# One row table for two mixture layers, and the first expert's first two slots made up in mid-attention

## The chip, the cores and the metric

The kernel runs on one NeuronCore of a Trainium2 chip. Its engines are TensorE (PE: matmuls, and the loads of their stationary operand, PEld), VectorE (DVE), ScalarE (ACT), GpSimd (POOL) and SyncE (SP), which only issues DMAs here; 16 DMA engines move the data. The metric is the device time of one execution in microseconds (us); of the kernel before there are three timed runs and one profiled execution.

## The reference

Three stages follow one another: attention with capped scores, a mixture of experts whose router knows the token's modality, and a second mixture without. Each token goes to one expert.

```python
scores = cap * np.tanh(scale * np.matmul(q, k.transpose(0, 1, 3, 2)) / cap)   # 4 batches, 12 heads, 448 tokens, 64 wide
attn = np.exp(scores - max); attn = attn / (attn.sum(-1, keepdims=True) + 1e-09)
x = np.matmul(attn, v)                       # then laid out as 1792 tokens x 768
# mixture 1 (mixture 2 is the same, without the bias)
logits = x @ w_gate + modality_bias[modality_id]
e_idx = np.argmax(logits, axis=1)            # 8 experts
gate_w = softmax(logits)[arange, e_idx]
for e in range(8):
    out[e_idx == e] = gate_w * (np.maximum(x[e_idx == e] @ w1[e], 0) @ w2[e])   # w1 768x1024, w2 1024x768
```

## The kernel before

**Attention.** Work goes by pairs of heads, 24 of them (4 batches x 6 pairs). `load(i)` issues five DMAs on SyncE for a pair: four pieces of Q and K into a tile `qkn` (pool `nat`, four buffers) and the values `vn`. In the loop over `i`, SyncE first gets the load of pair i+2. Then TensorE makes scores of pair i (L763, L767), ScalarE takes tanh and exp (L775, L777), and TensorE multiplies the exponentials of pair i-1 with its values (L811, L814) into the PSUM bank `po`, which VectorE copies to `ot` (L816). GpSimd and VectorE add up the exponentials (`presum`, `presum_last`). After each three pairs a `group` of tasks is put in a queue, one or two of which run between two pieces of a pair: the sums and router logits (L837), their transposes, the choice of expert, the rank of each token among its expert's tokens (`rank_a`), its place (`place_a`), and the transposes of `ot` into rows `xb`. `store` writes half of a batch's rows into a table in HBM, and `place_a` scatters token numbers by place into a list `td[0]`, so that the rows of an expert stand one after another there (four DMAs of 112 numbers from GpSimd, L963).

**Two row tables.** `xs[0]` takes the attention's rows, `xs[1]` the first mixture's results; each has 128 rows at its end that belong to no token. While the attention runs, SyncE copies such rows over the whole of `xs[1]` and over the last batch of `xs[0]` (L1004, L1007).

**Mixtures.** They go by slots: up to 128 tokens of one expert, gathered from the row table through the place list. A slot's x is transposed on TensorE (L329) and split into a high part `xh` and a low part `xl`; weights are split in the same way (`split_hi` on ScalarE, `split_lo` on VectorE or GpSimd, L285), and each product is three matmuls: high-high, high-low, low-high. `first(h, ks)` is the first layer for half h of the hidden width (L348 to L350), `second(h, ks)` the second (L368 to L370). While one slot is computed, the rows of the next are gathered (`load_tok` on SyncE, then `gather` on GpSimd, L323); `xg` holds one gathered tile.

**The junction.** The first expert is that of token 0, known after batch 0, and its weights come in mid-attention. `slot0` fills the expert's count up to 128 and loads its list after three batches, and its rows are gathered at the last pair. Behind the last pair's values, slot 0 is then computed piece by piece between the router steps of the last group, in an order written out by hand in the source. The place list gets the last batch there, and `slot_table` works out from the counts which expert and rows each slot has (`meta`, `nxt_i`, `beg_i`). `enter(0)` then loads the next expert's weights, finishes slot 0, transposes slot 1's x and gathers slot 2. All instructions of an engine run in this program order; each waits by semaphores. Of the DMAs that SyncE issues, each waits for the eighth before it.

Of the kernel before, what the change touches and what calls it, by code (L numbers as in the profile page):

```python
# [22 lines left out]
def tile_attention_two_moes(  # L23
# [37 lines left out]
    MAXS = NT + E  # L61
    SL = MAXS + 4
    LATE = 5
    FH = F // 2
# [10 lines left out]
    xs = [dram.tile([N + P, XW], F32, name=f"xs{l}") for l in range(2)]  # L75
# [12 lines left out]
    scol = cst.tile([P, 1], F32, name="scol")  # L88
    tokf = cst.tile([CP, B, NC], F32, name="tokf")
# [23 lines left out]
    def make_constants(tmp, none):  # L113
# [15 lines left out]
        iota(tokf, [[S, B], [1, NC]], 0, NC)  # L129
        iota(invf, [[0, 1]], N, 1)  # L130
        nc.gpsimd.iota(inv_i, pattern=[[0, ROWS // P + 1]], base=N, channel_multiplier=1)
        nc.gpsimd.iota(tok_i, pattern=[[S, B], [1, NC]], base=0, channel_multiplier=NC)
        iota(thr, [[P, NT]])
        iota(scol, [[0, 1]], 0, 1)
        iota(srow, [[1, SL + 1]])
# [10 lines left out]
        def none_rows():  # L146
            for l in range(2):
                nc.sync.dma_start(xs[l][N:N + P, :].rearrange("(p c) w -> p c w", c=NC), none)
                nc.sync.dma_start(td[l].rearrange("(p c) o -> p (c o)", p=P), inv_i)
# [20 lines left out]
    def fill_first(pool, cnt_ps, l, name):  # L170
# [8 lines left out]
        nc.vector.tensor_tensor(acc[l][0:1], acc[l][0:1], more, op=ALU.add)  # L179

# [122 lines left out]
    xg = cst.tile([P, XW], F32, name="xg")  # L303
    tk = cst.tile([P, 1], I32, name="tk")
    ti = cst.tile([P, 1], I32, name="ti")
# [13 lines left out]
    def gather(l, tk=tk, ti=ti):  # L319
        if tk is not None:  # L320
            nc.scalar.copy(ti, tk)
            pool_reads(ti)
        nc.gpsimd.indirect_dma_start(out=xg, out_offset=None, in_=xs[l],  # L323
                                     in_offset=bass.IndirectOffsetOnAxis(ap=ti, axis=0),
                                     bounds_check=N + P - 1, oob_is_err=False)
# [9 lines left out]
    def adopt(l, first=False):  # L335
        if not first:
            nc.vector.tensor_copy(gtc, gt1)
            if l:
                nc.vector.tensor_copy(tci, gtc[:, 1:2])
# [32 lines left out]
    def finish(l):  # L372
        nc.scalar.activation(yo[:, 0:DH], py[0][:, 0:DH], AF.Copy, scale=gtc[:, 0:1])  # L373
        nc.vector.tensor_scalar(yo[:, DH:D], py[1][:, 0:DH], gtc[:, 0:1], None, op0=ALU.mult)  # L374
        if l == 0:
            nc.vector.tensor_copy(tci, gtc[:, 1:2])
            nc.vector.tensor_copy(yo[:, D + 1:D + 2], gtc[:, 1:2])
            nc.vector.tensor_scalar(vm, gtc[:, 1:2], N - 0.5, None, op0=ALU.is_lt)
# [42 lines left out]
    def place(pk, gathered=False, copied=True):  # L421
# [5 lines left out]
        if gathered:  # L427
# [5 lines left out]
        nc.gpsimd.indirect_dma_start(out=xs[1], out_offset=bass.IndirectOffsetOnAxis(ap=t, axis=0),  # L433
                                     in_=y, in_offset=None, bounds_check=N - 1, oob_is_err=False)
# [191 lines left out]
    def enter(l):  # L626
# [4 lines left out]
        if l == 0:  # L631
            load_w1(0, e1, 2)
# [11 lines left out]
        with tc.If(reg(beg_i[l], 1, 1) == 1):  # L644
            for kk in range(KD):
# [629 lines left out]
```

## Time and profile before

| | us |
|---|---|
| median of the timed runs (lowest, highest) | 964.93 (962.68, 966.96) |
| profiled execution | 960.36 |
| its span, first to last instruction | 958.5 |
| TensorE busy (share of the span) | 902.5 (94%) |
| VectorE, ScalarE, GpSimd busy | 487.3 (51%), 432.8 (45%), 285.1 (30%) |
| mean granted clock of TensorE | 0.974 |

The page of the profile draws the span in 40 slices of 24 us. The first nine are attention, the tenth and eleventh hold its end and the first slots; the first mixture has 15 slots, the second 20. Each digit is the busy share of an engine in tenths; the row PEclk is the granted clock of TensorE, 1.0 being 2.4 GHz. In the 5th slice and around the 11th and 25th both TensorE and its clock are lower. The busy time of a stretch says little where several engines wait for one another; what ended each wait is in the lists of waits and in the order of time, of which the rows are below.

### The profile page before, as it was taken

The numbers are of one execution on the slowest core, as the hardware profiler recorded it, in microseconds if no ns is written. First come the engines' busy times: TensorE is split into PE (matmuls) and PEld (weight loads), VectorE is DVE, ScalarE is ACT, GpSimd is POOL, SyncE is SP. The second block draws the span as 40 slices with busy tenths as digits, with TensorE's granted clock in tenths as the row PEclk, the third lists the DMA queues.
The fourth block names the chain that finished last, engine by engine and source line by source line (L and its number), as shares of the span: only waits on it lengthen the run. The fifth ranks groups of instructions, "written<-read, shape, count | busy, mean of one in ns | idle before, by whom it ended". The sixth has DMA issues, their size and how long they took to land. (4 is left out here: it accounts for less than half of the span.)

```text
span 958.5 us, 15556 instructions
## 1 busy us (share of the span) xinstructions
PE 902.5 (94%) x4721; PEld 696.9 (73%) x4721; DVE 487.3 (51%) x1181; ACT 432.8 (45%) x666; POOL 285.1 (30%) x330
## 2 busy tenths in 40 slices
PE   8999899998599999999999985999999999999994
PEld 2333233334499899989989875899899989989984
DVE  3878468576633333394334564543612499952111
ACT  6787577785422222272222243533522488842121
POOL 7667457685412111112111220211111211211111
PEclk9999899998999999999999987999999999999998
DMA  8355998931574432275322335461811299981110
GB/s 186 99 182 125 149 297 153 287 46 47 68 260 54 37 46 34 34 205 135 45 37 35 53 85 194 138 248 36 311 38 35 77 337 375 370 330 35 51 51 20
DMA packets 59077, 128.11 MB, mean 134 GB/s; under 512 B 12920, under 2 KB 20072, under 8 KB 58602
## 3 DMA queue, kind: packets, MB, share of 16 engines
q1 hardware_dynamic: 51850, 100.68, 35.7%
q0 software_dynamic: 6960, 26.08, 13.8%
q14 instruction: 81, 0.66, 0.4%
q8 instruction: 42, 0.69, 0.3%
q10 hardware_dynamic: 144, 0.00, 0.0%
HBM read 109.27 MB, written 27.12 MB: 142 GB/s over the span
## 5 line engine op out<-in xcount | busy, mean ns | idle before, releaser
L368 PE MATMUL pb<-w2h,hh 128*128 128x384 f32 x560 | 193.6, 346 | 0.9 <-DVE meta L252 0.9
L369 PE MATMUL pb<-w2l,hh 128*128 128x384 f32 x560 | 189.0, 338 | 1.8 <-POOL w2l L285 1.6
L370 PE MATMUL pb<-w2h,hl 128*128 128x384 f32 x560 | 188.9, 337 | 0.0
L369 PEld LDWEIGHTS pb<-w2l,hh 128*128 128x128 f32 x560 | 106.2, 190 | 3.8 <-POOL w2l L285 2.0
L368 PEld LDWEIGHTS pb<-w2h,hh 128*128 128x128 f32 x560 | 106.2, 190 | 2.4 <-issue 1.2
L370 PEld LDWEIGHTS pb<-w2h,hl 128*128 128x128 f32 x560 | 106.0, 189 | 0.0
L775 ACT ACTIVATE tnh<-pa,rcap 128x896 f32<-128x896 f32 x72 | 70.0, 1005 | 53.4 <-PE pa L763 53.3
L361 DVE TENSOR_TENSOR hl<-pa,hh 128x512 fp32r<-128x512 f32 x34 | 23.5, 691 | 135.3 <-ACTq L480 130.2
L348 PE MATMUL po<-w1t,xh 128*128 128x512 f32 x210 | 87.8, 418 | 0.0
L348 PE MATMUL pa<-w1t,xh 128*128 128x512 f32 x210 | 85.4, 406 | 0.0
L349 PE MATMUL po<-w1t,xh 128*128 128x512 f32 x210 | 82.6, 393 | 1.6 <-DVEq L530 1.6
L349 PE MATMUL pa<-w1t,xh 128*128 128x512 f32 x210 | 83.6, 398 | 0.0
L350 PE MATMUL pa<-w1t,xl 128*128 128x512 f32 x210 | 83.4, 397 | 0.0
L350 PE MATMUL po<-w1t,xl 128*128 128x512 f32 x210 | 82.9, 395 | 0.0
L763 PE MATMUL pa<-qkn 64*128 64x448 f32 x288 | 71.5, 585 | 7.8 <-DMA qkn<-in_qk_dram 6.6
L777 ACT ACTIVATE prb<-tnh,capt 128x1792 f32<-128x1792 f32 (+1 forms) x48 | 77.0, 1604 | 3.2 <-ACT tnh L775 0.4
L373 ACT ACTIVATE yo<-pb,gtc 128x384 f32<-128x384 f32 x35 | 20.4, 583 | 121.2 <-PE pb L370 99.9
L285 DVE TENSOR_TENSOR w2l<-raw,w2h 128x768 fp32r<-128x768 f32 x77 | 70.4, 954 | 2.4 <-ACT w2h L279 1.7
L314 POOL TENSOR_TENSOR jki<-ti 128x1 int32<-128x1 int32 x35 | 7.5, 214 | 214.9 <-ACTq L516 128.1
L285 DVE TENSOR_TENSOR w1t<-raw,w1t 128x512 fp32r<-128x512 f32 x111 | 68.7, 687 | 3.1 <-ACT w1t L279 1.8
L314 POOL TENSOR_TENSOR jki<-pi 128x1 int32<-128x1 int32 x15 | 2.8, 184 | 226.5 <-DVE pi L424 175.3
L279 ACT ACTIVATE w1t<-raw 128x512 fp32r<-128x512 f32 x120 | 64.8, 623 | 0.4 <-ACTq L548 0.3
(287 smaller groups left out, 1560.7 us busy)
## 6 DMA issues: line engine op xcount, KB each, us to landing
raw<-in_w_dram SPq DMA_DIRECT2D x43, 1536.0 KB
qkn<-in_qk_dram SPq DMA_DIRECT2D x48, 128.0 KB
vn<-in_v_dram SPq DMA_DIRECT2D x24, 256.0 KB
xs<-xs SPq DMA_DIRECT2D x14, 385.0 KB
qkn<-in_qk_dram SPq DMA_DIRECT2D x48, 112.0 KB
xs<-xb SPq DMA_DIRECT2D x4, 672.0 KB
xs<-xb SPq DMA_DIRECT2D x3, 675.5 KB
xs<-xs SPq DMA_DIRECT2D x4, 336.9 KB
```

The costliest lines, as they stand in the source:

```text
L279: nc.scalar.activation(hi, raw[:, kk, :], AF.Copy)
L285: e.tensor_tensor(lo, raw[:, kk, :], hi, op=ALU.subtract)
L348: nc.tensor.matmul(ph[h], xh[:, kk, :], w1h(h, kk), start=kk == 0, stop=False)
L349: nc.tensor.matmul(ph[h], xh[:, kk, :], w1l(h, kk), start=False, stop=False)
L350: nc.tensor.matmul(ph[h], xl[:, kk, :], w1h(h, kk), start=False, stop=kk == KD - 1)
L361: nc.vector.tensor_tensor(hl[h], pt[h], hh[h], op=ALU.subtract)
L368: nc.tensor.matmul(o, hh[h][:, kk, :], w2h[h][:, kk, sl], start=h == 0 and kk == 0, stop=False)
L369: nc.tensor.matmul(o, hh[h][:, kk, :], w2l[h][:, kk, sl], start=False, stop=False)
L370: nc.tensor.matmul(o, hl[h][:, kk, :], w2h[h][:, kk, sl], start=False, stop=h == 1 and kk == 3)
L763: nc.tensor.matmul(ps[:, a, :], kn[r, ks], qn[r], start=True, stop=True)
L775: nc.scalar.activation(tv if w == 2 else tv[:, 0, :], ps, AF.Tanh, scale=rcap)
L777: nc.scalar.activation(p, t[:, 0:2 + w, :], AF.Exp, scale=capt)
```

## The change

- There is one row table `xs`: 128 rows of no token in front, then 1792 rows. The first mixture's results are written over the rows that the slots have read; gathers of the first mixture and these scatters are declared independent. The copies of L1004 and L1007 are gone, and token numbers in the lists are larger by 128.
- At pair 16 (`FILL`), `fill_two` fills the first expert's count up to two slots, from the two batches that have been placed. SyncE loads both lists at pair 17, GpSimd gathers slot 0 at pair 18, TensorE transposes it in pair 20 (`early_x`), and slot 1 is gathered at pair 21. Both gathers name only the rows of the first two batches.
- The first half of the first expert's w1 is split in pairs 15 to 20, one of six parts a pair, on ScalarE and VectorE; GpSimd splits no weights any more.
- `xh` and `xl` lie among the constants, and pool `nat` has three buffers instead of four. The last pair's values go to `po` like the others.
- The order between the last pair and slot 1 is written anew: three steps of the first layer come first; the slot table comes after the first layer. A slot more is allowed for (`MAXS`).

```diff
-    MAXS = NT + E
+    MAXS = NT + E + 1
+    FILL = 2 * NP + 4
-    xs = [dram.tile([N + P, XW], F32, name=f"xs{l}") for l in range(2)]
+    xs = dram.tile([P + N, XW], F32, name="xs")
+    read, written = [], []
...
+    def fill_two(pool, cnt_ps, name):
+        nc.tensor.matmul(cnt_ps, ones, acc[0], start=True, stop=True)
+        miss = pool.tile([2, E], F32, name=f"miss{name}")
+        nc.vector.tensor_scalar(miss, cnt_ps[0:2], -1.0, room, op0=ALU.mult, op1=ALU.add)
+        nc.vector.tensor_scalar(miss, miss, 0.0, float(P), op0=ALU.max, op1=ALU.min)
+        isf = pool.tile([2, E], F32, name=f"isf{name}")
+        nc.vector.tensor_scalar(isf, iota1[0:2], e1p[0][0:2], None, op0=ALU.is_equal)
+        more = pool.tile([2, E], BF16, name=f"more{name}")
+        nc.vector.tensor_tensor(more, miss, isf, op=ALU.mult)
+        nc.vector.tensor_tensor(acc[0][0:2], acc[0][0:2], more, op=ALU.add)
...
-    def gather(l, tk=tk, ti=ti):
+    def gather(l, tk=tk, ti=ti, rows=P + N):
...
+        if l == 0:
+            no_dep(d, written)
+            read.append(d.ins)
...
-        nat = early.enter_context(tc.tile_pool(name="nat", bufs=4))
+        nat = early.enter_context(tc.tile_pool(name="nat", bufs=3))
...
-                o_t[i] = (po if i < n - 1 else ph[0])[:, 0:S]
+                o_t[i] = po[:, 0:S]
...
+        def early_x(j):
+            if j:
+                adopt(0, True)
+            ks = slice(4 * j, min(4 * j + 4, KD))
+            w = ks.stop - ks.start
+            px = ps_t().rearrange("p (k c) -> p k c", c=P)[:, 0:w]
+            for kk in range(w):
+                nc.tensor.transpose(px[:, kk], xg[:, (4 * j + kk) * P:(4 * j + kk + 1) * P], ident)
+            nc.scalar.activation(xh[:, ks], px, AF.Copy)
+            nc.vector.tensor_tensor(xl[:, ks], px, xh[:, ks], op=ALU.subtract)
...
         for i in range(n):
             if i + 2 < n:
                 load(i + 2)
-            if 6 <= i < 6 + NT:
-                nc.sync.dma_start(xs[1][(i - 6) * P:(i - 5) * P, :], xs[0][N:N + P, :])
-                if i < 6 + NC:
-                    r = N - S + (i - 6) * CP
-                    nc.sync.dma_start(xs[0][r:r + CP, :], xs[0][N:N + CP, :])
+            if i == FILL + 1:
+                r0 = reg(row0_i[0], 0, ROWS - N, engines=SP)
+                load_tok(0, r0)
+                load_tok(0, r0 + P, tkb)
...
-                if i == n - NP + 1:
-                    def slot0():
-                        fill_first(rt, ps_t()[:, 0:E], 0, "a")
-                        load_tok(0, reg(row0_i[0], 0, ROWS - P, engines=SP))
-                    queue.append(slot0)
-            if i == n - 1:
-                gather(0, None, tk)
+            if i == FILL:
+                fill_two(rt, ps_t()[:, 0:E], "a")
+            if i == FILL + 2:
+                gather(0, None, tk, P + 2 * S)
+            if i == FILL + 5:
+                gather(0, None, tkb, P + 2 * S)
+            if 0 <= i - FILL + 1 < KD:
+                split_w1(0, i - FILL + 1)
...
+                if i == FILL + 4:
+                    early_x(c // 2)
...
-        x_transpose()
-        x_split()
-        adopt(0, True)
-        for kk in range(4, KD):
-            split_lo(raw1[0], w1h(0, kk), w1l(0, kk), kk, "p")
-        t_sums()
+        first(0, range(3))
         for kk in range(KD):
             split_hi(raw1[1], w1h(1, kk), kk, "a")
-        split_lo(raw1[1], w1h(1, 0), w1l(1, 0), 0, "v")
-        for kk in (1, 2, 3):
-            split_lo(raw1[1], w1h(1, kk), w1l(1, kk), kk, "p")
+        t_sums()
+        for kk in range(2):
+            split_lo(raw1[1], w1h(1, kk), w1l(1, kk), kk, "v")
...
-        first(0, range(2))
+        first(0, range(3, 5))
         t_scalars()
-        first(0, range(2, 4))
-        for kk in range(2):
-            split_hi(raw2[0], w2h[0][:, kk, :], kk, "a")
+        first(0, range(5, 6))
+        relu(0)
         rows_[0](True)
-        first(0, range(4, 6))
         choose_()
-        relu(0)
+        for kk in range(2, 4):
+            split_lo(raw1[1], w1h(1, kk), w1l(1, kk), kk, "v")
+        first(1, range(1))
...
+        for kk in range(4):
+            split_w2(0, kk)
+        first(1, range(3, 6))
         relu(1)
+        st = slot_table(mc, px[:, 6:8, :].rearrange("p a b -> p (a b)"), 0)
+        next(st)
+        second(0, range(1))
+        next(st)
+        second(0, range(1, 2))
+        h_transpose(1)
+        h_split(1)
```

What the change moves on TensorE behind the last pair. Before, from the last pair's values on (`pa_120` is their bank, `xg` slot 0's rows, the rows with `one_h`, `wgp` and `one_a` are the last group's sums):

```order
L811 MATMUL pa_120<-prb,vn 64x448 x6
L814 MATMUL pa_120<-prb,vn 128x448
L329 MATMUL pa_119<-ident,xg 128x128 x6
L837 MATMUL pb_122<-pst,one_h 32x448 x2
L837 MATMUL pb_122<-prb,one_h 32x448
L837 MATMUL pb_122<-ot,wgp 32x448 x2
L837 MATMUL pb_122<-psm,one_a 32x448 x2
L837 MATMUL pb_122<-ot,wgp 32x448
L348 MATMUL pa_120<-w1t_0_110,xh 128x512
```

And in the changed kernel, where the same lines have other numbers (L841 and L844 are the values, L375 to L377 the first layer, L867 the sums):

```order
L841 MATMUL po<-prb,vn 64x448 x6
L844 MATMUL po<-prb,vn 128x448
L375 MATMUL pa_120<-w1t_0_110,xh 128x512
L376 MATMUL pa_120<-w1t_3_113,xh 128x512
L377 MATMUL pa_120<-w1t_0_110,xl 128x512
L375 MATMUL pa_120<-w1t_0_110,xh 128x512
L376 MATMUL pa_120<-w1t_3_113,xh 128x512
L377 MATMUL pa_120<-w1t_0_110,xl 128x512
```

Slot 0's transposes no longer stand between the values and the sums, and nine matmuls of its first layer do.

On SyncE, around the store of the second half of batch 0, that is the loads of pairs 12 and 13. Before (`qkn` and `vn` are a pair's load, `xs_63<-xs_62` the copy between the tables):

```order
L906 DMA xs_62<-xb 448x1x386
L696 DMA qkn<-in_qk_dram 64x448
L697 DMA qkn<-in_qk_dram 64x512
L696 DMA qkn<-in_qk_dram 64x448
L697 DMA qkn<-in_qk_dram 64x512
L699 DMA vn<-in_v_dram 128x512
L1004 DMA xs_63<-xs_62 16x6160
L696 DMA qkn<-in_qk_dram 64x448
```

And in the changed kernel:

```order
L936 DMA xs<-xb 448x1x386
L726 DMA qkn<-in_qk_dram 64x448
L727 DMA qkn<-in_qk_dram 64x512
L726 DMA qkn<-in_qk_dram 64x448
L727 DMA qkn<-in_qk_dram 64x512
L729 DMA vn<-in_v_dram 128x512
L726 DMA qkn<-in_qk_dram 64x448
```

The copy has gone from the queue; store and loads keep their order.

On VectorE, behind the copy of the last pair's values. Before (`xl`, `gt` are slot 0's split and gate column, `ls` the last group's sums, `w1t_3` a low part of w1's second half):

```order
L816 COPY ot<-pa_120 128x448
L333 TENSOR_TENSOR xl<-pa_119,xh 128x768
L340 COPY gt_130<-xg 128x2
L843 COPY ls<-pb_122 96x448
L285 TENSOR_TENSOR w1t_3_1747<-raw_1_107,w1t_0_1744 128x512
L852 TENSOR_SCALAR rd<-pb_123,eps 112x24
```

And in the changed kernel:

```order
L846 COPY ot<-po 128x448
L873 COPY ls<-pb_121 96x448
L302 TENSOR_TENSOR w1t_3_1752<-raw_1_107,w1t_0_1749 128x512 x2
L882 TENSOR_SCALAR rd<-pb_122,eps 112x24
L883 RECIPROCAL rd<-rd 112x24
```

The split of x and its gate column left this place, and a second low part, GpSimd's before, came to it.

## Rows read from the trace of the kernel before

**Rows 1.** What TensorE waited for: us in total, times, longest us.

```profile
PE pa L329 <- DMA xg<-xs,tk: 12.2, 2, 7.8
...
PE pa L763 <- DMA qkn<-in_qk_dram: 6.6, 4, 2.6
```

**Rows 2.** Order of time, TensorE: start, us, engine, line, operation, [idle before]; junction and slot 1.

```profile
220.21 2.48 PE L811 MATMUL pa<-prb,vn 128*64 128x448 f32 x12
...
227.96 1.54 PE L329 MATMUL pa<-ident,xg 128*128 128x128 f32 x6 [4.33 <-DMA xg<-xs,tk]
...
263.35 1.54 PE L329 MATMUL pa<-ident,xg 128*128 128x128 f32 x6 [7.85 <-DMA xg<-xs,tk]
...
269.04 0.39 PE L348 MATMUL pa<-w1t,xh 128*128 128x512 f32 x1
...
283.58 0.82 PE L329 MATMUL pa<-ident,xg 128*128 128x128 f32 x6
```

**Rows 3.** Order of time, TensorE, pairs 12 and 13.

```profile
108.86 0.99 PE L763 MATMUL pa<-qkn 64*128 64x448 f32 x2 [2.00 <-DMA qkn<-in_qk_dram]
112.45 3.32 PE L763 MATMUL pa<-qkn 64*128 64x448 f32 x6 [2.60 <-DMA qkn<-in_qk_dram]
...
116.73 3.26 PE L811 MATMUL po<-prb,vn 128*64 128x448 f32 x8
...
127.28 1.72 PE L811 MATMUL po<-prb,vn 128*64 128x448 f32 x8
```

**Rows 4.** Stretches: length, busy us of five engines, granted clock, DMA share, GB/s.

```profile
98.00:100.00 2.00, 2.00 (x14) 0.99 (x11) 1.47 (x6) 0.97 (x2) 2.00 (x3) 1.00 1.10 21
110.00:120.00 10.00, 7.55 (x20) 2.75 (x20) 3.04 (x5) 3.81 (x3) 1.89 (x2) 0.51 0.87 230
180.00:200.00 20.00, 20.00 (x97) 7.73 (x92) 15.82 (x30) 15.67 (x16) 11.89 (x7) 1.00 0.68 194
220.20:269.00 48.80, 33.96 (x165) 24.18 (x165) 28.70 (x85) 20.64 (x52) 25.38 (x21) 0.86 0.41 82
225.60:256.00 30.40, 24.88 (x126) 17.46 (x126) 22.26 (x73) 17.24 (x44) 19.34 (x15) 0.89 0.42 60
228.00:234.40 6.40, 6.40 (x23) 2.26 (x23) 3.30 (x2) 4.86 (x9) 6.20 (x6) 0.60 0.35 109
263.30:267.30 4.00, 3.95 (x15) 3.95 (x16) 1.20 (x3) 0.89 (x2) 0.19 (x1) 0.50 0.57 147
```

**Rows 5.** Order of time, SyncE's DMA issues.

```profile
92.59 0.58 SPq L906 DMA_DIRECT2D xs<-xb  x1
...
95.64 0.60 SPq L696 DMA_DIRECT2D qkn<-in_qk_dram  x1
...
97.54 0.50 SPq L1004 DMA_DIRECT2D xs<-xs  x1
...
256.33 0.36 SPq L317 DMA_DIRECT2D tk<-td  x1
```

**Rows 6.** Order of time, VectorE, the last copy of the attention.

```profile
224.98 0.62 DVE L816 COPY ot<-pa 128x448 f32<-128x448 f32 x1
```

**Rows 7.** VectorE's groups from 225.6 to 256 us: count, busy us, mean ns.

```profile
L285 DVE TENSOR_TENSOR w2l<-raw,w2h 128x768 fp32r<-128x768 f32 x5 | 4.6, 941 | 0.0
L230 DVE TENSOR_SCALAR live<-srow,tot 1x26 int32<-1x26 f32 x1 | 3.2, 3225 | 0.0
L340 DVE COPY gt<-xg 128x2 f32<-128x2 f32 x1 | 2.4, 2421 | 0.0
L285 DVE TENSOR_TENSOR w1t<-raw,w1t 128x512 fp32r<-128x512 f32 x3 | 1.9, 672 | 0.0
L333 DVE TENSOR_TENSOR xl<-pa,xh 128x768 fp32r<-128x768 f32 x1 | 1.0, 958 | 4.8 <-ACT xh L332 4.8
```

**Rows 8.** Order of time, GpSimd: the scatter of the last batch's places, slot 1's gather.

```profile
244.87 1.79 POOL L963 DMA_INDIRECT td<-tok_i,pi  x1 [0.30 <-issue]
...
259.15 1.05 POOL L323 DMA_INDIRECT xg<-xs,tk  x1 [8.86 <-DMA tk<-td]
```

More of the change, by code (lines that the diff above doesn't have):

```diff
@@ L88, in tile_attention_two_moes @@
     scol = cst.tile([P, 1], F32, name="scol")
+    room = cst.tile([2, 1], F32, name="room")
     tokf = cst.tile([CP, B, NC], F32, name="tokf")
@@ L303, in tile_attention_two_moes @@
     xg = cst.tile([P, XW], F32, name="xg")
+    xh = cst.tile([P, KD, P], F32R, name="xh")
+    xl = cst.tile([P, KD, P], F32R, name="xl")
     tk = cst.tile([P, 1], I32, name="tk")
+    tkb = cst.tile([P, 1], I32, name="tkb")
     ti = cst.tile([P, 1], I32, name="ti")
@@ L322, in gather, with no_dep @@
             pool_reads(ti)
-        nc.gpsimd.indirect_dma_start(out=xg, out_offset=None, in_=xs[l],
-                                     in_offset=bass.IndirectOffsetOnAxis(ap=ti, axis=0),
-                                     bounds_check=N + P - 1, oob_is_err=False)
+        d = nc.gpsimd.indirect_dma_start(out=xg, out_offset=None, in_=xs[0:rows],
+                                         in_offset=bass.IndirectOffsetOnAxis(ap=ti, axis=0),
+                                         bounds_check=rows - 1, oob_is_err=False)
+        if l == 0:
+            no_dep(d, written)
+            read.append(d.ins)
+    def no_dep(d, others):
+        for o in others:
+            tc.declare_no_dep(d.ins, o, reason="a token is in one slot, and its row written once that slot is computed")
     def x_transpose():
@@ L338, in adopt @@
             if l:
-                nc.vector.tensor_copy(tci, gtc[:, 1:2])
+                nc.vector.tensor_scalar(tci, gtc[:, 1:2], -float(P), None, op0=ALU.add)
         nc.vector.tensor_copy(gt1, xg[:, D:D + 2])
@@ L643, in enter @@
                 load_tok(l, r2)
-        with tc.If(reg(beg_i[l], 1, 1) == 1):
-            for kk in range(KD):
-                split_w1(0, kk)
-            load_w1(0, reg(nxt_i[l], 1, 2 * E - 1, engines=SP))
+            with tc.If(reg(beg_i[l], 1, 1) == 1):
+                for kk in range(KD):
+                    split_w1(0, kk)
+                load_w1(0, reg(nxt_i[l], 1, 2 * E - 1, engines=SP))
         nsl = reg(meta[l], M_N, MAXS, lo=1)
@@ L1108, in tile_attention_two_moes @@
         w2h.append(mc.tile([P, KF // 2, D], F32R, name="w2h1"))
-        first(1, range(3, 4))
-        for _ in st:
-            pass
-        load_tok(0, reg(meta[0], M_ROW + 1, ROWS - P, engines=SP))
-        load_w1(0, reg(nxt_i[0], 0, 2 * E - 1, engines=SP), 0, 2)
-        first(1, range(4, 6))
-        relu(1)
-        for kk in (2, 3):
-            split_lo(raw2[0], w2h[0][:, kk, :], w2l[0][:, kk, :], kk, "pvpv"[kk])
-        gather(0, None, tk)
-        for kk in range(1):
+        for kk in range(4):
+            split_w2(0, kk)
+        first(1, range(3, 6))
+        relu(1)
+        st = slot_table(mc, px[:, 6:8, :].rearrange("p a b -> p (a b)"), 0)
[5 more added lines that the diff above has]
+        h_split(1)
+        for kk in range(2):
             split_hi(raw2[1], w2h[1][:, kk, :], kk, "a")
@@ L1152, in tile_attention_two_moes @@
     yo = gp.tile([P, XW], F32, name="yo")
-    second(0, range(2))
-    h_transpose(1)
     for kk in range(4):
+        if kk >= 2:
+            split_hi(raw2[1], w2h[1][:, kk, :], kk, "a")
+        split_lo(raw2[1], w2h[1][:, kk, :], w2l[1][:, kk, :], kk, "v")
         if kk == 1:
-            h_split(1)
-        if kk >= 1:
-            split_hi(raw2[1], w2h[1][:, kk, :], kk, "a")
-        split_lo(raw2[1], w2h[1][:, kk, :], w2l[1][:, kk, :], kk, "vvpv"[kk])
+            for _ in st:
+                pass
     def slots(l, nsl, e1):
```

63 lines of the change are left out of this document (22 added, 41 removed).

## The prediction

> **What bounds the kernel now.** Read first the list of what TensorE waited for, then TensorE's own order of time around each wait, then the same moments on the DMA queue, VectorE and GpSimd. TensorE is busy in nearly all of the span, so only its idle time and its time at half clock can be won, and the list says where they lie. In the stretch that the change touches there are two causes [rows 1]. Scores of the attention wait 6.6 us, in four pieces, for the Q and K of their pair. The transposes of a gathered x tile wait 12.2 us in two pieces for rows gathered with `tk`: 4.33 us between the last pair and slot 0, and 7.85 us between slot 0 and slot 1 [rows 2].
>
> Each wait is followed by half clock. After the two scores' waits at 108.9 and 112.5 us, eight value matmuls take 3.26 us, and a pair later 1.72 [rows 3]; the stretch from 110 to 120 us has a granted clock of 0.51, which is the 1.2 GHz level for nearly all of it. After the first gather's wait, 228 to 234.4 us runs at 0.60, and after the second, 263.3 to 267.3 at 0.50 [rows 4].
>
> Why Q and K come late: SyncE issues the store of half a batch at 92.59, the third and fourth Q/K pieces of pair 12 from 95.64, a copy of 385 KB inside the row tables at 97.54 [rows 5]; the second wait for them ends at 112.45 [rows 3], 16.8 us after their issue. In between the DMA engines are taken and move little: share 1.10 and 21 GB/s from 98 to 100 us, against 0.68 and 194 GB/s over 180 to 200 [rows 4].
>
> **The junction, from the last pair's values to the end of slot 0.** It lasts from 220.21 (values) to 269.04 (slot 1's first layer), 48.8 us [rows 2]. TensorE is busy 33.96 of the 48.80 us measured [rows 4], so 14.8 are idle. Of the busy time, 6.40 x 0.40 = 2.6 and 3.95 x 0.50 = 2.0 are what half clock cost. The six transposes of slot 0's x move into the attention, 0.8 at full clock. If TensorE never waited, the piece would be 33.96 - 2.6 - 2.0 - 0.8 = 28.6 us: the gain is at most 20.2.
>
> It will wait, because VectorE is late next. GpSimd's nine low parts of w1 and three of w2 go: six of w1 into the attention, the other three w1 and three w2 to VectorE behind the last pair. VectorE's last copy of the attention ends at 225.6 [rows 6] and it was busy 22.26 us from there to 256 [rows 4]. It loses the split of slot 0's x and the copy of its gate column (the latter a long one, 2.42) and gains 3 x 0.67 + 3 x 0.94 = 4.8 [rows 7]: 22.3 - 1.0 - 2.4 + 4.8 = 23.7. To that I add 5.5 us in which it must wait in the new order: 2.8 for the sums of the last group (they need the copy that ends at 225.6; before, with most of slot 0's transposes, they filled the 6.40 us at 0.60 [rows 4], 3.8 at full clock), 0.8 for their transposes, 1.4 for slot 0's hidden transposes behind ScalarE, 0.5 for small ones. VectorE then ends at 225.6 + 23.7 + 5.5 = 254.8 on the old clock, and TensorE has six second-layer matmuls, about 1 us, behind the last split: 255.9. The row `live`, 3.23 us for 26 numbers [rows 7], is an outlier that need not come again; I count a small part of it out and take 255.5. So the gain of the junction is 269.0 - 255.5 = **13.5 us**, between 7.7 (only the wait before slot 0 goes: 4.33 + 2.6 + 0.8) and 20.2 (TensorE never waits).
>
> **Slot 2's gather.** Slot 1's rows are there early, but slot 2's now come by the chain that slot 1's came by. That chain, as it stands: the last of four scatters of the last batch's places is issued at 244.87, its place list can be read only at 256.33 [rows 5, 8], the gather is issued 2.8 us later at 259.15 [rows 8] and its transposes start 4.2 us after that [rows 2]. Behind the change the scatters leave some 6 us sooner, but the list waits for the slot table, whose last VectorE part I put at 253 to 254; list at 254, gather at 257, landing at 261 if nothing is in front. Two weight loads of 1.5 MB are issued right behind the list, and at the 194 to 230 GB/s of [rows 4] 3.1 MB take 13 to 16 us, so a landing at 270 is the bad case. It is wanted 14.5 us after slot 1 begins (269.04 to 283.58 before [rows 2]), at 255.5 + 14.5 = 270. I take a loss of **0.5 us**, between 0 and 4.3, the length of the first gather's wait.
>
> **The attention.** What goes: 18 copies between row-table parts, one fill of 385 KB, and so the copy that shares the engines with pair 12's Q and K. At stake are the 6.6 us of waits and 7.55 x 0.49 = 3.7 us at half clock from 110 to 120 [rows 1, 4]: 10.3. The store stays in front of pair 12's loads, so I leave 1.5 of the waits and count the clock back: 8.8.
>
> What comes: six transposes of slot 0's x, 0.8; the count matmul with its three small vector steps, 0.2; six weight splits, each 0.6 on ScalarE and 0.67 on VectorE [rows 7]; two activations and two subtractions for x. The cover is idle time: in 180 to 200 us ScalarE is busy 15.67 of 20 and VectorE 15.82, while TensorE is busy all 20 [rows 4]. The two value rows of [rows 3] are a pair and 10.55 us apart, of which some 1.7 are half clock, so a pair is about 8.8 us and has some 1.9 us free on both engines, and a split takes 0.7. If the cover fails, because a split stands ahead of the copy that empties the value bank, each of the six costs its whole 0.67: 4. I take 0.3 for all six. Both gathers, on GpSimd, take 1 us each beside 11.89 of 20 busy; what stands behind them there is the pair's partial sums, wanted only by the group's sums a pair later. The list loads on SyncE stand ahead of two loads of the pair two ahead and of the last weight load, and wait for scatters issued more than a pair before; I cost them at nothing, and at 1 us once if the landing takes the 9.7 us between 246.7 and 256.3 [rows 5, 8]. Net: 8.8 - 1.3 = **7.5 us**, between -4 (waits stay, splits uncovered) and 10.3.
>
> Fewer buffers for Q and K (three, not four): the load of pair i+2 may start only when the scores of pair i-1 are done, about two and a quarter pairs or 19.8 us ahead. Five issues take 3 us, so a load has 16.8 us to land: plenty for most, and just what pair 12's took. I count nothing, and it is a rival below.
>
> **The rest.** Running the reference's routing on its inputs, the first token's expert gets 456 tokens in the first two batches, so the two slots are full of real tokens, no filler enters, and the layer keeps its 15 slots and the next its 20. In the slots the gathers and scatters wait for the same things as before; the table grows by one number. Nothing.
>
> **Sum.** 7.5 + 13.5 - 0.5 = 20.5 us. The profiled execution took 960.36 (span 958.5): 939.9. The runs' median is 964.93, 4.57 above it, so the forecast for the median is 944.4, said as **944**. About 0.5%, 4.8 us, is what can be told from no change.
>
> **A rule that speaks against the attention's part.** The 21 GB/s at a share of 1.10 [rows 4] can have another cause than the copy. The Trainium skill, "DMA: Bandwidth & Descriptors", section "Specifications", says that transfers under 512 B become read-modify-writes and miss line rate; a batch's 448 places are scattered as single 4-byte numbers right beside the store. By that rule the slow stretch stays, and the sum is the first rival's; the trace shows the slow landing of such scatters (9.7 us above) but does not say which of the three is to blame.
>
> **Rivals.**
> - *The loads stay late.* Store and scatters, which stay, make pair 12 wait, not the copies. For: the store is first in the queue. Against: the wait ends 16.8 us after the issue, long for one store. Attention -1 instead of 7.5, total 12: 953. Chance 0.16.
> - *The junction keeps a wait of several microseconds.* VectorE carries all that GpSimd did, or slot 2's gather is late, and the clock falls again. Junction 7.7: total 7.5 + 7.7 - 0.5 = 14.7: 950. Chance 0.11. With both together 958 or more, within 0.5 to 0.9% of before: no change, chance 0.05.
> - *Slower: three buffers are too few.* If every load were as slow as pair 12's and the list loads ahead of it added 2 us, each of 21 pairs would wait 2 us: 42, less the 20 won: 987. It decides from about 1 us per pair, where it eats the 20. Against: four waits in 24 pairs, and the copies are gone from the queue. Chance 0.04.
> - Forecast, 937 to 950: 0.64.
>
> From these: faster by over 0.5%: 0.91; within: 0.05; slower: 0.04. The range takes in both first rivals and, below, both terms at their best (20.2 + 10.3 = 30.5, 934): **932 to 957**.
>
> **What would show it.** Right: no wait for Q and K above 1 us, behind the stores too, and the clock full through the attention; first-layer matmuls follow the last values with no gap; the junction is 33 to 37 us long, with TensorE's small waits there ended by VectorE; slot 1's transposes wait for nothing. Wrong: scores still wait for Q and K after each store; a gather's wait at slot 2; VectorE late by more than its 23.7 us of work; or half clock behind the last pair.

## The result, and the profile after

The changed kernel takes 955.78 us (median of four runs, 954.37 to 956.86), the kernel before 963.80 beside it (962.34 to 966.96): a ratio of 0.989, 95% interval 0.986 to 0.993, so 7 to 13 us are won, and 10 is the best single figure. The forecast was 944 within 932 to 957. The profiled execution has a span of 952.3 us against 958.5 and a granted clock of 0.977 against 0.974.

Two profiles can be laid side by side at marks that both have (the last pair's values, the first matmul of slot 1, ScalarE's `yo` of each slot):

| stretch | before | after | difference |
|---|---|---|---|
| start to the last pair's values | 220.21 | 217.07 | -3.1 |
| values to slot 1's first layer (the junction) | 48.83 | 36.03 | -12.8 |
| slot 1 | 20.94 | 24.68 | +3.7 |
| slots 2 to 13 | 246.02 | 247.75 | +1.7 |
| last slot, turn, first slot of mixture 2 | 62.65 | 64.34 | +1.7 |
| the rest of mixture 2 | 359.85 | 362.43 | +2.6 |
| span | 958.5 | 952.3 | -6.2 |

The junction came as forecast (13.5). The attention gave less than half of its 7.5, and 9.7 us were lost behind the junction, where the forecast had 0.5. The first row isn't sharp: a second profile of the kernel before (r1) has 224.67 there, and five profiles with the changed kernel's attention have 216.37 to 221.49, so what the attention gave is not told closer than nothing to 8 us.

The list of TensorE's waits in the changed kernel (total, times, longest), the answer to [rows 1]:

```profile
PE pa L356 <- DMA xg<-xs,ti: 10.0, 1, 10.0
PE pa L793 <- DMA qkn<-in_qk_dram: 3.9, 1, 3.9
PE pa L624 <- DVE acc L452: 3.0, 1, 3.0
PE pb L424 <- ACT prod L418: 2.7, 1, 2.7
...
PE pb L424 <- DMA wgt<-in_moe_w_gate_dram: 2.0, 1, 2.0
PE pa L218 <- DVE bn L216: 2.0, 1, 2.0
PE pb L188 <- DVE acc L991: 1.7, 1, 1.7
```

The 12.2 us for rows gathered with `tk` are gone (the 10.0 with `ti` is the turn to mixture 2, in both kernels). Q and K still cost 3.9. New are the waits for the router weights `wgt`, for `bn` at the slot table and, in `fill_two`, for `acc` (L188). Two of the kernel before have grown: for `prod` in the last slot (2.7, before 0.4) and for `acc` in the turn (3.0, before 1.7). TensorE's order of time through the junction, the answer to [rows 2]:

```profile
217.07 2.48 PE L841 MATMUL po<-prb,vn 128*64 128x448 f32 x12
219.47 1.02 PE L844 MATMUL po<-prb,vn 128*128 128x448 f32 x2
219.98 0.74 PE L375 MATMUL pa<-w1t,xh 128*128 128x512 f32 x1
...
240.71 0.17 PE L218 MATMUL pa<-bn,ones 128*128 128x16 bf16 x1 [2.02 <-DVE bn L216]
...
249.29 0.81 PE L356 MATMUL pa<-ident,xg 128*128 128x128 f32 x6
...
253.10 0.39 PE L375 MATMUL pa<-w1t,xh 128*128 128x512 f32 x1
...
263.38 1.50 PE L424 MATMUL pb<-wgt,prod 128*128 128x8 f32 x12 [2.03 <-DMA wgt<-in_moe_w_gate_dram]
...
271.56 0.82 PE L356 MATMUL pa<-ident,xg 128*128 128x128 f32 x6
```

The first layer follows the values without a gap, the largest wait of the junction is ended by VectorE, and the transposes of slot 1 (249.29) and of slot 2 (271.56) wait for nothing. In between stands the wait for `wgt`. Pair 12's wait, the answer to [rows 3], and the new one in pair 16:

```profile
109.75 3.09 PE L793 MATMUL pa<-qkn 64*128 64x448 f32 x6 [3.88 <-DMA qkn<-in_qk_dram]
...
147.60 0.17 PE L188 MATMUL pb<-acc,ones 128*128 128x8 bf16 x1 [1.70 <-DVE acc L991]
```

The stretches of [rows 4] in the changed kernel (us, then busy time of PE, PEld, DVE, ACT, POOL, granted clock, DMA share, GB/s):

```profile
243.70:248.70 5.00, 5.00 (x18) 5.00 (x18) 4.93 (x19) 2.64 (x4) 0.00 (x0) 0.50 0.01 1
265.75:269.30 3.55, 3.55 (x12) 3.36 (x11) 1.21 (x5) 0.78 (x3) 0.00 (x0) 0.52 0.91 355
92.00:96.00 4.00, 4.00 (x18) 1.21 (x18) 2.69 (x5) 1.34 (x2) 3.38 (x4) 1.00 1.42 118
96.00:100.00 4.00, 4.00 (x22) 1.76 (x20) 2.39 (x8) 2.88 (x4) 4.00 (x3) 1.00 0.73 19
110.00:115.30 5.30, 5.30 (x14) 2.83 (x16) 0.64 (x1) 2.65 (x3) 0.00 (x0) 0.50 0.74 194
```

Three waits are each followed by 1.2 GHz: pair 12's (110 to 115.3), VectorE's at the slot table (243.7 to 248.7) and that for `wgt` (265.75 to 269.3). And 96 to 100 us is as slow as before, 19 GB/s, without any copy in the queue. SyncE's issues there and at slot 1, the answer to [rows 5]:

```profile
91.61 0.61 SPq L936 DMA_DIRECT2D xs<-xb  x1
92.30 0.58 SPq L726 DMA_DIRECT2D qkn<-in_qk_dram  x1
...
95.31 0.59 SPq L727 DMA_DIRECT2D qkn<-in_qk_dram  x1
...
249.30 0.99 SPq L288 DMA_DIRECT2D raw<-in_w_dram  x2
251.69 0.34 SPq L337 DMA_DIRECT2D tk<-td  x1
252.09 0.43 SPq L1188 DMA_DIRECT2D wgt<-in_moe_w_gate_dram  x1
```

Pair 12's load still stands behind the store of half a batch (91.61), and `wgt` is issued behind two weight loads of 1.5 MB. VectorE's last copy of the attention and its last split of w2 before slot 1:

```profile
221.84 0.62 DVE L846 COPY ot<-po 128x448 f32<-128x448 f32 x1
...
247.53 1.81 DVE L302 TENSOR_TENSOR w2l<-raw,w2h 128x768 fp32r<-128x768 f32 x2
```

### The profile page after: what moved, and what is told of

Same layout as the page of the kernel before. It is cut to its first block, busy times and chain, and to the rows that moved or that the text cites. A ratio compares the mean times of both kernels' runs of the same rounds, so it can differ in the third digit from the quotient of the medians.

```text
span 952.3 us, 15519 instructions
## 1 busy us (share of the span) xinstructions
PE 904.0 (95%) x4721; PEld 702.2 (74%) x4721; DVE 494.9 (52%) x1196; ACT 432.4 (45%) x667; POOL 267.3 (28%) x318
## 5 line engine op out<-in xcount | busy, mean ns | idle before, releaser
L395 PE MATMUL pb<-w2h,hh 128*128 128x384 f32 x560 | 195.7, 349 | 0.0
L396 PE MATMUL pb<-w2l,hh 128*128 128x384 f32 x560 | 191.7, 342 | 0.6 <-issue 0.4
L375 PE MATMUL po<-w1t,xh 128*128 128x512 f32 x210 | 88.5, 421 | 0.0
L375 PE MATMUL pa<-w1t,xh 128*128 128x512 f32 x210 | 85.0, 405 | 0.0
L377 PE MATMUL po<-w1t,xl 128*128 128x512 f32 x210 | 84.5, 402 | 0.0
L377 PE MATMUL pa<-w1t,xl 128*128 128x512 f32 x210 | 83.1, 396 | 0.0
L302 DVE TENSOR_TENSOR w1t<-raw,w1t 128x512 fp32r<-128x512 f32 x120 | 77.9, 713 | 3.3 <-ACT w1t L296 1.7
L302 DVE TENSOR_TENSOR w2l<-raw,w2h 128x768 fp32r<-128x768 f32 x80 | 73.0, 954 | 2.9 <-ACT w2h L296 2.1
L841 PE MATMUL po<-prb,vn 128*64 128x448 f32 x288 | 65.0, 560 | 0.9 <-DVE ot L846 0.9
```

The lines of the kernel that those rows point to most:

```text
L302: e.tensor_tensor(lo, raw[:, kk, :], hi, op=ALU.subtract)
L375: nc.tensor.matmul(ph[h], xh[:, kk, :], w1h(h, kk), start=kk == 0, stop=False)
L377: nc.tensor.matmul(ph[h], xl[:, kk, :], w1h(h, kk), start=False, stop=kk == KD - 1)
L395: nc.tensor.matmul(o, hh[h][:, kk, :], w2h[h][:, kk, sl], start=h == 0 and kk == 0, stop=False)
L396: nc.tensor.matmul(o, hh[h][:, kk, :], w2l[h][:, kk, sl], start=False, stop=False)
L841: nc.tensor.matmul(o_t[i][a * HD:(a + 1) * HD, :], vn[:, c, a, :], p[:, 2 * (c % 2) + a, :], start=c == 0, stop=False)
```

## The experiments

All ratios are to the kernel before on the same chip; the changed kernel has 0.989 (0.986 to 0.993). r1 and r10 are not in the table: each is a single execution, taken for its profile.

| run | ratio | 95% interval |
|---|---|---|
| r2 store behind the load | 0.980 | 0.975 to 0.984 |
| r3 scatters later | 0.980 | 0.975 to 0.984 |
| r4 copies kept | 0.992 | 0.989 to 0.995 |
| r5 slot 1's rows late | 0.997 | 0.993 to 1.000 |
| r6 w1 splits late | 0.994 | 0.990 to 0.998 |
| r7 router weights first | 0.986 | 0.979 to 0.992 |
| r8 tiles on 64 B | 0.988 | 0.982 to 0.995 |
| r9 fill half a pair later | 0.989 | 0.985 to 0.993 |
| r11 three together | 0.976 | 0.974 to 0.978 |
| r12 the three, tiles as before | 0.975 | 0.973 to 0.978 |

### What makes pair 12 late

```diff
-            ends += [lambda: store(b, DH, XW)]
+            ends += [lambda: owed.append(b)]
...
             if i + 2 < n:
                 load(i + 2)
+            while owed:
+                store(owed.pop(), DH, XW)
```

> The changed kernel, with the store of a batch's second half issued behind the Q/K load of the next pair instead of ahead of it. Theory 'the store in front of the load makes pair 12 late': pair 12's wait of 3.9 us falls under 0.5, the half clock behind it (110 to 115.3 us) goes, 4 to 6 us are won against the changed kernel, about 950 to 952. Rival 'the small scatters of the batch's places hold the engines': the load still lands late, the wait stays above 2 us. Rival 'it only moves': pair 12 is on time and pair 13, whose load now follows the store, waits 3 us or more; the time stays at 955 to 957.

```diff
+            if b == 0:
+                held.append((b, pi))
+            else:
+                scatter(b, pi)
...
+                if c and held and i == NP + 4:
+                    scatter(*held.pop())
```

> The changed kernel, with the four scatters of the first batch's places issued one pair later, so that they no longer lie beside the store and pair 12's load. Theory 'store': pair 12's wait stays within 1 us of 3.9 and the slow stretch (16 to 21 GB/s from 96 to 100 us) stays. Rival 'scatters': the store and the load run at over 150 GB/s, the wait falls under 1 us and 4 to 6 us are won, 950 to 952.

```diff
+            if 6 <= i < 6 + NT:
+                nc.sync.dma_start(idle[(i - 6) * P:(i - 5) * P, :], xs[0:P, :])
+                if i < 6 + NC:
+                    nc.sync.dma_start(idle2[r:r + CP, :], xs[0:CP, :])
```

> The changed kernel with the 18 copies of rows of no token issued where they were issued before, now into two tables that nothing reads. It isolates what the copies cost in the attention. Theory 'the copies cost little, store and scatters are in the way in any case': pair 12's wait grows from 3.9 to at most 6.6 with pair 18's back at about 3, 2 to 4 us in all, 958 to 960. Rival 'the copies were what the forecast took them for': 7 us or more, 963 or above. Rival 'nothing': within 1 us of 955.8.

First exponential of pairs 11 and 12 on ScalarE, in the changed kernel and in r2:

```profile
100.70 1.79 ACT L807 ACTIVATE prb<-tnh,capt 128x1792 f32<-128x1792 f32 x1
114.67 1.79 ACT L807 ACTIVATE prb<-tnh,capt 128x1792 f32<-128x1792 f32 x1
```

```profile
100.87 1.79 ACT L807 ACTIVATE prb<-tnh,capt 128x1792 f32<-128x1792 f32 x1
109.00 1.79 ACT L807 ACTIVATE prb<-tnh,capt 128x1792 f32<-128x1792 f32 x1
```

14.0 us have become 8.1. In r3 too pair 12 starts on time (108.65). Each of the two edits ends the wait by itself; the windows, of r2 and then of r3, say how store and scatters work together:

```profile
92.00:96.00 4.00, 4.00 (x17) 1.28 (x18) 2.69 (x5) 1.18 (x2) 3.37 (x4) 1.00 1.59 119
96.00:100.00 4.00, 4.00 (x22) 1.65 (x20) 2.22 (x8) 2.88 (x4) 4.00 (x3) 1.00 0.56 10
```

```profile
92.00:96.00 4.00, 4.00 (x18) 1.08 (x14) 3.25 (x5) 1.53 (x2) 1.89 (x2) 1.00 0.80 230
96.00:100.00 4.00, 4.00 (x22) 1.77 (x21) 2.40 (x8) 2.88 (x4) 2.80 (x3) 1.00 0.76 229
```

Without the scatters the store and the load behind it run at 230 GB/s. With them the DMA engines are taken for 0.56 to 0.73 of the time and move 10 to 19 GB/s from 96 to 100 us, in r2 as well; only there the load of pair 12 had gone ahead (its last piece is issued at 87.50, in the changed kernel at 96.01) and nobody waits. So pair 12 is late when four scatters of 112 single numbers run beside the store and the load stands behind it, where SyncE issues it only when VectorE has finished the half batch. What isn't shown is whether the scatters need the store to slow the load so much: no run puts them beside the load without it. In r3 they are issued from 99.95 us on, beside loads, and 104 to 108 us moves 124 GB/s at a share of 1.21. And beside the second batch's store, with four scatters as well, the changed kernel moves 93 and then 170 GB/s (152 to 160 us), so what makes the first stretch so deep stays open.

In r4, with the copies back in the queue, there are these waits, the second and third of them not in the changed kernel's profile:

```profile
109.58 1.83 PE L795 MATMUL pa<-qkn 64*128 64x448 f32 x2 [3.71 <-DMA qkn<-in_qk_dram]
112.30 2.58 PE L795 MATMUL pa<-qkn 64*128 64x448 f32 x5 [0.89 <-DMA qkn<-in_qk_dram]
...
170.50 1.74 PE L795 MATMUL pa<-qkn 64*128 64x448 f32 x6 [1.52 <-DMA qkn<-in_qk_dram]
```

By the ratio the copies cost 0.3%, about 3 us, with intervals that overlap, so "nothing" isn't excluded, and the 7 us of the second theory are not borne out. The attention ends at 223.32 us in r4's profile and at 216.37 to 221.49 in the five profiles with the changed kernel's attention. The first theory fits, but its details aren't shown to be the copies': pair 12's 4.6 us lie within the 3.6 to 4.8 of the profiles that have its wait and no copies, and pair 18 waits without copies too in r6 (1.3) and r9 (1.7). That the copies were not the cause of pair 12's wait is shown.

### The junction

```diff
-                load_tok(0, r0 + P, tkb)
...
-            if i == FILL + 5:
-                gather(0, None, tkb, P + 2 * S)
...
             for _ in st:
                 pass
+            load_tok(0, reg(meta[0], M_ROW + 1, ROWS - P, engines=SP), tkb)
+            gather(0, None, tkb, P + 2 * S)
```

> The changed kernel, but slot 1's list and rows are fetched behind the slot table at the junction, as the kernel before did, and not mid-attention; slot 0 stays early. Theory 'early rows are what the junction gained': the transposes of slot 1 wait 7 to 10 us for the rows, half clock follows, and 8 to 12 us of the junction's 12.8 are gone, with a little back where the list of slot 2 then has more time: 962 to 966 where the changed kernel has 955.8. Rival 'the junction is bound by VectorE in any case, the rows are hidden': within 2 us of 955.8.

```profile
258.52 1.51 PE L356 MATMUL pa<-ident,xg 128*128 128x128 f32 x6 [10.23 <-DMA xg<-xs,tkb]
```

The wait is back, longer than before (7.85 in [rows 2]), and half clock behind it. Slot 0 ends 10.8 us later than in the changed kernel; 3.8 come back in slot 1, where `wgt` has then landed. The ratio says 7 us: 963 where the changed kernel has 955.8, within the 962 to 966 expected. The early rows are most of what the junction gained.

```diff
-            if 0 <= i - FILL + 1 < KD:
-                split_w1(0, i - FILL + 1)
...
+        for kk in range(KD):
+            split_hi(raw1[0], w1h(0, kk), kk, "a")
         presum_last(n - 2)
...
+        for kk in range(4):
+            split_lo(raw1[0], w1h(0, kk), w1l(0, kk), kk, "p")
         for c in range(NC):
             values(n - 1, c)
```

> The changed kernel, but the six high parts of the first half of w1 are made on ScalarE and the six low parts on GpSimd around the last pair, as before, and not mid-attention on ScalarE and VectorE. Theory 'splits in the attention are hidden there and would stand on the path at the junction': pairs 15 to 20 keep their 8.8 to 10 us, the first layer waits 3 to 6 us behind the last values, half clock follows, 3 to 7 us are lost: 959 to 963. Rival 'they cost in the attention what they win': within 1.5 us of 955.8, and the attention ends 2 us earlier.

```profile
226.02 0.56 PE L867 MATMUL pb<-pst,one_h 128*32 128x448 f32 x1 [1.59 <-DVE pst L831]
```

Values to slot 0's end take 38.2 us instead of 35.7, and TensorE waits for VectorE's part of the last group's sums. In the attention pair 15 (from its first exponential to the next pair's) is 0.74 us shorter without a split, 9.29 against 10.03. Pair 19 is shorter by 0.68, but that isn't the split's: in r3, r5, r8 and r9, with the split, it takes the same 9.1 us. The other four are not shorter. What this run shows is the junction's 2.5 us, the sign that the theory expected and just under its range. The ratio's 4 us don't show more: the interval overlaps that of the changed kernel, and slot 1 takes 27.9 us here as it does in r3 and r8, which don't have this edit (below).

### Slot 1 and the router weights

```diff
-            nc.sync.dma_start(wgt, w_gate2t.rearrange("(k p) e -> p k e", p=P))
...
+    nc.sync.dma_start(wgt, w_gate2t.rearrange("(k p) e -> p k e", p=P))
     n0, e1 = enter(0)
```

> The changed kernel, with the load of the second layer's router weights issued ahead of the list of slot 2 and the two 1.5 MB weight loads instead of behind them. Theory 'queued behind 3 MB': the 2.03 us wait of slot 1's logits goes, and with it most of the half clock from 265.75 to 269.3; slot 1 to slot 2 falls from 25.0 us to 21 or 22; 2.5 to 4 us are won, 952 to 953. Rival 'another wait is behind it' (rows of slot 2, VectorE's choice of the expert): the logits no longer wait and slot 1 takes as long, within 1 us of 955.8.

SyncE's issue and the logits in that run:

```profile
236.52 0.57 SPq L1231 DMA_DIRECT2D wgt<-in_moe_w_gate_dram  x1
```

```profile
259.52 1.40 PE L424 MATMUL pb<-wgt,prod 128*128 128x8 f32 x12
```

No wait any more. From `yo` to `yo`, slot 1 takes 24.8 to 27.9 us in the eight profiles of the changed kernel and its variants that have the wait (1.8 to 4.2 us long), and 20.3, 20.3 and 21.3 in the three with this edit (r7, r11, r12). The theory holds: 3.5 us or more, though the ratio of this run alone could not tell it.

### The fill

```diff
-            if i == FILL:
-                fill_two(rt, ps_t()[:, 0:E], "a")
...
+                if i == FILL and c == 2:
+                    fill_two(rt, ps_t()[:, 0:E], "a")
```

> The changed kernel, with the count matmul and its vector steps that fill up the first two slots put half a pair later in pair 16, behind the value matmuls of its first half. Theory 'TensorE stands 1.70 us at the count matmul because VectorE has not yet added the second batch's counts': that wait goes, pair 16 (10.0 us from its first exponential to pair 17's in the changed kernel) falls to 8.1 to 8.5, 1.5 to 1.9 us won, 954. Rival 'the pair is bound by VectorE, whose copies and sums are the same': the wait is taken over by the value matmuls for the emptied bank or by the sums, within 0.7 us of 955.8.

```profile
154.15 0.17 PE L188 MATMUL pb<-acc,ones 128*128 128x8 bf16 x1
...
164.19 0.99 PE L793 MATMUL pa<-qkn 64*128 64x448 f32 x2 [1.74 <-DMA qkn<-in_qk_dram]
```

The wait for `acc` goes and the pair (15 as counted here, 16 in the expectation) is 1.9 us shorter, but pair 18 now comes before its Q and K and waits, with half clock behind it. The time is unchanged: the rival is right that the gain is taken over, by a wait that it didn't name. A second thing that takes it over is seen in r11, under "Together".

### The spacing of the slots

> The kernel before, unchanged, for a second profile of it. Behind the junction the changed kernel's slots were slower by a little: 20.55 us apart in the middle of the first layer against 20.475, and 18.36 in the second against 18.235. Theory 'it is the kernel' (the x tiles lie elsewhere in memory): this run repeats 20.475 and 18.235 within 0.03, and the variants of the changed kernel sent with it repeat 20.55 and 18.36. Rival 'it is the execution': this run's spacing differs from the first profile's by as much as 0.1, and no order of the kernels by spacing holds.

```diff
+    pad0 = cst.tile([P, 8], F32, name="pad0")
     xh = cst.tile([P, KD, P], F32R, name="xh")
...
     gtc = cst.tile([P, 2], F32, name="gtc")
+    pad1 = cst.tile([P, 8], F32, name="pad1")
...
+    pad2 = gp.tile([P, 8], F32, name="pad2")
     w2l.append(gp.tile([P, KF // 2, D], F32R, name="w2l1"))
```

> The changed kernel with three unused pads of 32 B per partition, so that xh, xl (now at odd multiples of 32 B) and the low half of w2's second part begin at a multiple of 64 B, as they did before; nothing else moves in order. In the second layer a slot is 18.36 us in the changed kernel's profiles and 18.23 in both of the kernel before, some 1.5 ns on every matmul. Theory 'place of the tiles': 18.23 again, and 20.48 in the first layer in place of 20.57; 17 x 0.13 + 12 x 0.09 = 3.3 us won, 952.5. Rival 'not the tiles' (the code, or the table in DRAM): 18.33 to 18.36 stay and the time is within 1 us of 955.8.

> As the run before with pads (slots of the second layer 18.29, first layer 20.49), but the first pad ahead of the raw weights, so that raw weights, the first half of w1's parts and the x row begin at odd multiples of 32 B too: every tile that TensorE reads in the slots lies as in the kernel before, modulo 64 B. Theory 'place of the tiles, all of it': 18.23 and 20.48. Rival 'half is the tiles, half something else (the code, the larger table)': 18.29 stays.

ScalarE's `yo` at two neighbouring slots of mixture 2, of the kernel before, the changed one, and r12 (the pads of r10):

```profile
653.43 0.58 ACT L373 ACTIVATE yo<-pb,gtc 128x384 f32<-128x384 f32 x1 [4.73 <-PE pb L370]
671.66 0.58 ACT L373 ACTIVATE yo<-pb,gtc 128x384 f32<-128x384 f32 x1 [1.59 <-issue]
```

```profile
645.18 0.58 ACT L400 ACTIVATE yo<-pb,gtc 128x384 f32<-128x384 f32 x1 [4.78 <-PE pb L397]
663.54 0.58 ACT L400 ACTIVATE yo<-pb,gtc 128x384 f32<-128x384 f32 x1 [1.65 <-POOL jki L334]
```

```profile
636.71 0.58 ACT L402 ACTIVATE yo<-pb,gtc 128x384 f32<-128x384 f32 x1 [4.75 <-PE pb L399]
654.98 0.58 ACT L402 ACTIVATE yo<-pb,gtc 128x384 f32<-128x384 f32 x1 [1.62 <-issue]
```

18.23 us, 18.36 and 18.27. Within a kernel the spacing repeats to 0.02 over seventeen slots but for one, which is 0.08 longer in every profile, and the second profile of the kernel before (span 965.3, another execution) has 18.23 again: it belongs to the kernel. It is not a wait, since TensorE has no gap in such a slot in either: laid side by side, the starts of its matmuls drift apart by 0.06 us over the second half of the first layer and by 0.05 over the last four microseconds, and hardly in between. With the pads of r8 the spacing is 18.29, with those of r10, of which the first stands ahead of the raw weights, 18.27; both lie between the theory and its rival. In mixture 1 slots 2 to 13 take 247.0 to 247.2 us with pads (r8, r10, r12), 247.75 in the changed kernel, and 246.0 and 246.7 in the two profiles of the kernel before, which r1 thus doesn't repeat there. So where tiles begin, modulo 64 B, makes half to two thirds of the difference in mixture 2; r12 against r11, which differ in the pads alone, has 0.06 of 0.10. The pads move every tile behind them, and which of them counts is not separated; that it is TensorE's operands is argued. The rest stays open: r4 and r11, with the tiles of the changed kernel, have 18.33, and what differs in them is the order of some instructions and, in r4, two tables in HBM. In r8's time the 2 us are lost among other differences.

### Together

> The changed kernel with three edits together: the half-batch store behind the next pair's Q/K load, the router weights ahead of the expert weights, the fill half a pair later. Alone they gave, as ratios to the kernel before, 0.980, 0.986 and 0.989 where the changed kernel has 0.989. Theory 'three separate causes': the gains add where each removes a wait of its own, 9 + 3.5 + 2 (the last now that pair 18's load no longer queues behind the store) = 14.5 us, ratio 0.974 +- 0.003; pair 16 takes 8.1 to 8.5 us, no wait for Q and K over 0.5, no wait for the router weights. Rival 'waits replace one another': the fill's gain is again taken by a wait for Q and K at pair 18, or slot 1 waits elsewhere, ratio 0.978 or more.

> The run before with the pads that put TensorE's tiles where the kernel before had them, modulo 64 B. In the single profile with these pads a slot of the second layer was 18.27 us against 18.36 and of the first 20.51 against 20.55: 17 x 0.09 + 12 x 0.05 = 2.1 us. Theory 'the tiles': 18.27 again, 2 us under the run before, ratio 0.972. Rival 'the spacing of that run was its own': 18.36, the same time as the run before within 0.5 us in the profile behind the junction.

r11 is at 944.55 us where the kernel before has 968.79. No score waits for Q and K and nothing waits for `wgt`. But the fill gave nothing again: the attention ends at 210.78 us, in r2 without that edit at 210.49. Pair 15 is 1.9 us shorter here too, but pairs 18 and 19 are 2.8 longer than in r2. TensorE in pair 18 of r11:

```profile
159.70 1.72 PE L841 MATMUL po<-prb,vn 128*64 128x448 f32 x8 [1.68 <-DVE ot L846]
```

An addition of router logits on VectorE, in the changed kernel and then in r11:

```profile
158.97 1.27 DVE L898 TENSOR_TENSOR lg<-bias,lr 112x32 f32<-112x32 f32 x1
```

```profile
149.64 5.18 DVE L898 TENSOR_TENSOR lg<-bias,lr 112x32 f32<-112x32 f32 x1
```

GpSimd beside it, and its wait behind it, in r11:

```profile
149.51 1.16 POOL L831 TENSOR_TENSOR pst<-pst,prb 128x448 f32<-128x448 f32 x1
150.61 2.10 POOL L818 TENSOR_TENSOR psm<-psm,prb 128x896 f32<-128x896 f32 x1
152.65 2.10 POOL L814 TENSOR_TENSOR psm<-prb 128x896 f32<-128x896 f32 x1
159.13 1.14 POOL L831 TENSOR_TENSOR pst<-pst,prb 128x448 f32<-128x448 f32 x1 [4.37 <-DVE pst L830]
```

This addition of 112x32 numbers takes 5.15 to 5.18 us in the three runs with the later fill (r9, r11, r12) and 0.8 to 2.4 in all eleven other profiles. In r11 it ends with the last of three GpSimd additions that follow one another without a pause. (The Trainium skill, "SBUF — State Buffer", section "SBUF: two separate sides", says that a VectorE operation with two SBUF inputs and a GpSimd one that reads SBUF use one pair of ports, which the one that starts first holds for its whole instruction; the rows agree, though it is not said there that VectorE stands through three in a row.) GpSimd then stands 4.37 us for VectorE's sums and TensorE 1.68 for VectorE's copy. By these rows the two engines, which wait for each other's partial sums, take back what the fill won; no run moves that addition, so it is not tested by itself. So the gains that add are two, 0.9% for the store and 0.3% for the router weights, by the ratios 0.976 together; the rival was right about the third. r12 differs from r11 by nothing that the times can tell (0.975 and 0.976); its slots of mixture 2 are 18.27 us again, as its theory had it, against 18.33 in r11, and from the first slot of mixture 2 to the end its profile is 1.1 us shorter, not the 2 expected.

## Why the prediction was partly right

- **Junction, 13.5 us: right**, 12.8. No gap behind the values, slot 1's rows there in time, VectorE the one that TensorE waits for. r5 shows that the early rows carry it, r6 that the early splits do some 2.5. That the size came so close is in part luck: VectorE's last split ended 26.9 us behind its last copy of the attention, where the prediction had 29.2, and the half clock, which it put at nothing, made up for that. One of the signs of error that it named, half clock behind the last pair, did come: five microseconds at 0.50 behind VectorE's wait at the slot table, some 2.5 us.
- **Attention, 7.5 us: the step that failed.** "The copy that shares the engines with pair 12's Q and K" was taken for the cause, so its removal was to leave 1.5 of 6.6 us of waits and full clock. The profile after has 3.88 us and half clock again, and r3 shows what is to blame: the scatters beside the store, which the change keeps. Of pair 12's 4.6 us of waits 0.7 went; pair 18's 2.0 are gone from the profile. The rival that the loads stay late was right. What the Trainium skill says of small transfers ("DMA: Bandwidth & Descriptors", section "Specifications"), weighed there, is said of these transfers themselves. What the prediction drew from it, that the slow stretch stays, is what the trace shows (230 GB/s without the small scatters, 118 and 19 with them). The argument used against this rival, that 16.8 us are long for one store, was the very sign of it. And "each wait is followed by half clock" is not so behind pair 18's two waits of 1 us in the kernel before, where 168 to 184 us has a granted clock of 1.00; the sum did not use it.
- **The fill, 0.2 us: 1.9, with the split of its pair.** The matmul and three vector steps were costed as work. What counts is when the counts that they read are there: VectorE adds the second batch's just then, and TensorE stood 1.70 us with the next pair's scores behind it. Taking the wait away won nothing, though, since Q and K (r9) and VectorE beside GpSimd (r11) were late a little later.
- **Slot 2's gather, 0.5 us: nothing**, no wait at 271.56. But the queue was looked at for the list and the rows alone. The router weights stand in the same queue behind the same 3 MB, and they were 2 to 4 us late. The 13 to 16 us that the prediction itself worked out for these loads would have shown it.
- **The six splits, 0.3 us: 0.7**, in pair 15, as r6 shows, and these are part of the 1.9 above; five were hidden. **Three buffers, nothing: right** in the profile after, where no pair but 12 waits for Q and K. In the variants without copies pair 18 waits up to 1.7 us, which is less than the 2.0 and 3.7 that it waits in two profiles of the kernel before, with four.
- **"The rest: nothing": wrong by some 4 us.** Slots 2 to 13 and mixture 2 became slower by 0.14 us a slot, of which half to two thirds in mixture 2 is that tiles moved by 32 B. The last slot and the turn take 61.1 to 66.0 us in the variants of the changed kernel and 62.6 in both profiles of the kernel before. In all of the former the last slot's logits wait 2.6 to 3.5 us for ScalarE's `prod`, in the latter 0.4 and 0.5; why, and what else differs, wasn't settled.

By what was measured the sum is 3.1 + 12.8 - 3.7 - 1.7 - 1.7 - 2.6 = 6.2 us for the two profiled executions, and other executions would share it out otherwise. The time lies in the range by 1.2 us, and that is owed to the range's width: of the 20.5 us that the sum had, some 10 came.

## What to carry to other kernels

Before a DMA is blamed for a slow stretch, list everything that is under way there with its piece size: a few hundred single numbers beside a large store took the engines to a twelfth of their rate and less, and moving either of the two away won 9 us, where deleting 7 MB of copies won some 3, or nothing. When a chain is moved forward, look at each DMA in the queue behind it, also those whose consumer was never late: its deadline has moved too. And give a wait removed its worth only after asking which pair of engines is late next.

## What was not expected of the hardware

- 448 numbers scattered from GpSimd beside a 676-KB store: 118 and then 19 GB/s over 8 us at a DMA share of 1.42 and 0.73, against 230 and 229 without them.
- Pads of 32 B, which change where tiles begin modulo 64 B, are worth 0.06 to 0.09 us in 18.3 of unbroken matmuls, some 0.3 to 0.5%.
- A VectorE addition of 112x32 numbers took 5.2 us beside three GpSimd additions in a row (r11) and 1.27 in the changed kernel.
